# The first unit's first phase in token halves: gate/up of 256 tokens, their down projection with the convolution's tasks, then the other 256

## Chip, cores, metric

The kernel runs on one core of a Trainium2 chip. The metric is device time in microseconds (us); smaller is better. All matrices are bfloat16, sums are float32.

## What is computed

Four layers in a row on x = A_q, of shape (2048 tokens, 576 channels). Layers 1 and 3 are a long convolution with gating, layers 2 and 4 a gated feed-forward network with 4608 hidden channels:

```python
def _A_ref(q, k, v, shift_k, ssm_k, ssm_D):      # q is the layernorm of x
    k_shift = sum over t < 4 of k_pad[:, t:t + S, :] * shift_k[:, 3 - t]
    kv = k_shift * v
    y = causal convolution over the 2048 tokens of kv with ssm_k, per channel (by FFT)
    y = y + kv * ssm_D
    return q * y

def _B_ref(x, w_gate, w_up, w_down):             # x is the layernorm of x
    return (_gelu(x @ w_gate) * (x @ w_up)) @ w_down

x = x + _A_ref(_layernorm(x), A_k, A_v, A_shift_k, A_ssm_k, A_ssm_D)
x = x + _B_ref(_layernorm(x), B_w_gate, B_w_up, B_w_down)
x = x + _A_ref(_layernorm(x), A_k, A_v, A_shift_k, A_ssm_k, A_ssm_D)
x = x + _B_ref(_layernorm(x), B_w_gate, B_w_up, B_w_down)
```

The convolution's result y does not depend on x, so it is computed once, for both convolution layers.

## The kernel before

**Units and phases.** Tokens are taken in four blocks of 512. A unit is one feed-forward layer on one block; there are eight: for each pair of blocks, layer 2 on both and then layer 4 on both. A unit has three phases, each over a third of the hidden channels (12 tiles of 128). A phase is *gate/up* (for each tile, 18 matmuls of 64 rows, gate and up side by side in the array, L1848; half as many columns at a time in the first phase, L1684), the product gelu(gate) * up into the hidden tile `hT` (gelu on ScalarE, L1663 or L1857; the product on VectorE, L1667, L1690 or L1858), and *down* (`down_rows`: for each of four rows of 128 tokens, 24 matmuls of 128 rows and 288 columns, L1723), whose sum is added to `x_c` on VectorE (L1759, L1762, L1754).

**The convolution.** It is done by matrices of 128 x 128 in blocks of 512 tokens: forward transforms on TensorE (in quarters, `quarter`, L284, copied out by ScalarE, L287, and combined by VectorE, L247, L251, L256), products with the filter's transform on VectorE (L361 to L364, L622), and inverse transforms on TensorE (`inverse`, L417, copied to `y` by ScalarE, L423). The opening (`begin`) does the first block; the work of the later blocks is cut into tasks that a planner sets between the feed-forward's instructions. One convolution pair takes a PSUM tile from the pool `cps` (one tile) or, when the planner allows it, from the pool `ps` (three tiles, tag `pr`), which gate/up, down and the transpositions share.

**What sets the order.** The order of every engine's instructions is fixed when the program is built. A planner (`Pace`, `fill`, `run_v`, `run_p`) keeps a modelled time for TensorE, VectorE and ScalarE, with the constants `C_...`, and puts a task in where its inputs should be ready. The constant `H1_AT` is the modelled time from which the transform of the second filter block may begin. Each engine runs its own list in order and waits on semaphores. DMAs are issued from SyncE (weights `wgu` and `wd`, and the transposes of `xn` into `xnT`, L1341) and from GpSimd (the rest).

**The first phase of the first unit** (`wb == 0`). Its input `xnT` comes from transpositions on TensorE (`turn0`, L1483), copied out by ScalarE or VectorE (`copy0`, L1490). Tokens stand in `xnT` in the order `AT0 = (0, 2, 1, 3)`, so that rows 0 and 2, ready first, make the first 256 tokens. `first_half` does gate/up of these for all 12 tiles, in six blocks of two tiles (`half_gu`, 36 matmuls), and sets the transpositions of rows 1 and 3 and the first convolution tasks between the blocks. Then six blocks do the other 256 tokens, with convolution tasks between them, and then `down_rows` does all four rows, with more convolution tasks.

**The second unit's input.** The first inverse transform after the opening (L417, in the first unit's third phase) gives y of the second block. VectorE forms x plus the gated y (L1279, L1286), ScalarE its sum of squares (L1244), GpSimd the root (L1251, L1252), VectorE the norm `xn` (L1316, L1318), and SyncE issues two transposes for each of the four rows into `xnT` (L1341). The second unit's gate/up needs all eight.

**Scratch.** `begin` has its scratch in a pool `s_tmp`, which is closed at its end. The pools of `hT` and of `wd` (down's matrix, a sixth of it in each of three buffers) are opened after it and take its place, so the first three loads of `wd` (L1208) wait for the last readers of that scratch.

Of the kernel before, what the change touches and what calls it, by code (L numbers as in the profile page):

```python
# [15 lines left out]
ACT = mybir.ActivationFunctionType  # L16
# [6 lines left out]
P = 128  # L23
# [8 lines left out]
FG = 4  # L32
NEVER = 1e9

C_GU, C_DN = 1.944, 0.245
C_PR = 1.25
C_BF, C_TB, C_R4 = 0.41, 0.46, 0.77
C_SQ, C_TINY, C_NA, C_NV, C_ROOT, C_NB = 0.85, 0.6, 0.95, 0.74, 1.5, 0.4
# [2 lines left out]
C_TT, C_ST, C_HT, C_H2, C_GELU, C_EVA, C_EVD = 0.76, 0.82, 0.69, 0.7, 0.6, 0.66, 0.76  # L41
LAG = 0.25
AHEAD, CHAINED = 2.0, 2.5
H1_AT = 13.0
LATE = (1, 2)
HOLD, LEAD, HURRY, SPARE = 14.0, 1.8, 2.6, 4.0
LANDED, ENDING, VISIT, EARLY = 9.0, 1.5, 1.6, 1.6
# [40 lines left out]
class Conv:  # L88
# [755 lines left out]
    def begin(self, head, tables):  # L844
# [4 lines left out]
        with ExitStack() as es:  # L849
# [3 lines left out]
            sk9 = tmp.tile([NH, 2, HP * KS], BF16, name="sk9")  # L853
            dv9 = tmp.tile([NH, 2, HP], BF16, name="dv9")
            sk9t = tmp.tile([NH, KS, HP], BF16, name="sk9t")
            hx = tmp.tile([P, RT, D], BF16, name="hx")
            dcol = tmp.tile([P, nd + 1], F32, name="dcol")
            nt = nd - 1
            DW = D - nt * P
            wcol = tmp.tile([P, nt, KS], F32, name="wcol")  # L860
            sx = tmp.tile([P, KS, DW], BF16, name="sx")
            warm = tmp.tile([P, 1], F32, name="warm")
            self.Wx = tmp.tile([P, 2, P], BF16, name="Wx")
            Wn = tmp.tile([P, 2, P], BF16, name="Wn")
            hn = tmp.tile([P, nd + 1, BS], BF16, name="hn")
            hT0 = tmp.tile([P, RT, D], BF16, name="hT0")
            kT = head.scratch([P, nt, RT, P + 2], "kT")
            dg = head.scratch([P, nt, RT, P], "dg")
            kx = tmp.tile([P, RT + KS - 1, DW], BF16, name="kx")
# [9 lines left out]
            nc.vector.memset(kT[:, :, :, 0:2], 0.0)  # L879
            nc.vector.memset(below[:, 0:1], 0.0)  # L880
            nc.vector.tensor_copy(out=below[:, 1:P], in_=self.ident[:, 0:P - 1])
            nc.scalar.activation(out=warm[:], in_=full[:, 0:1], func=ACT.Sqrt)
# [5 lines left out]
            nc.sync.dma_start(out=self.Wx[:], in_=tables[:, 24:26, :])  # L888
# [4 lines left out]
            nc.sync.dma_start(out=self.Td[1].rearrange("(t p) d -> p t d", p=P), in_=hx[:])  # L893
            head.more(2)

            new = lambda: self.psp.tile([P, 2, 512], F32, tag="pr", name="ps")
# [229 lines left out]
            nc.scalar.activation(out=warm[:], in_=head.zero, func=ACT.Gelu_apprx_tanh)  # L1126
            self.keep_y(0, 3, Y[3])
            head.stats(3)
            self.load_v(1, nc.gpsimd)
# [11 lines left out]
def ssm_geglu_kernel(ctx, tc, A_q, A_k, A_v, A_shift_k, A_ssm_k, A_ssm_D, B_x, B_w_gate, B_w_up,  # L1141
# [308 lines left out]
    with tc.manual_schedule():  # L1450
# [136 lines left out]
        def more(k):  # L1587
# [7 lines left out]
        head = SimpleNamespace(  # L1595
            zero=neghalf_t[:], more=more, reserve=reserve0, idle=idle0, stats=stats0, act_stats=act_stats0, half_stats=half_stats0, root_of=root_of0, mean_of=mean_of0, scales=scales0, even_out=even_out0, gate_even=gate_even0, gate=gate0, mean=mean0, sq=sq0, std=std0, norm=norm0, turn=turn0, copy=copy0,
            scratch=lambda shape, name: xtp.tile(shape, BF16, tag="xnT", name=name),
            stay=lambda: xpool.tile([P, RT, 2, D], BF16, tag="x", name="H1"))
        conv.begin(head, tables)

        first_pools = ctx.enter_context(ExitStack())
        hpool = first_pools.enter_context(tc.tile_pool(name="hT", bufs=1))
        dpool = first_pools.enter_context(tc.tile_pool(name="wd", bufs=3))
        for n in range(3):
            load_wd(n)

        def first_half(hT):

            gvars[0][1]["rstd"] = small.tile([P, 1], F32, tag="e_rstd", name="rstd")
            nc.vector.reciprocal(out=gvars[0][1]["rstd"][:], in_=gvars[0][1]["std"])  # L1610
            gate0(1, None, 1)
            mean0(1)
            gate0(3)
            mean0(3)
            for n in range(FP // 2):
                tail = half_gu(hT, n, 0, n < 4)
                t.pe += C_GU
                if n == 3:
                    t.on_dve(C_HT, t.on_act(C_GELU, t.pe + 0.15) + 0.15)
                if n == 0:  # L1620
                    sq0(1)
                    root0(1)
                if n < 4:
                    tail()
                if n == 0:
                    norm0(1)
                if n == 1:
                    sq0(3)
                    conv.put_at(0)
                    root0(3)  # L1630
                elif n in (2, 3, 4):
                    if n == 2:
                        norm0(3)
                        for part, kt in ((1, 0), (0, 1), (1, 1)):
                            conv.apart0(conv.A0, part, kt)
                        conv.together0(conv.A0)
                        conv.put_at(1)
                        load_x(1)
                        t.dve, t.act = t.pe + 3.4, t.pe + 0.6
                    if n < 4:  # L1640
                        conv.run_p()
                    if n > 2:
                        j = 2 * n - 5
                        turn0(j)
                        copy0(j, nc.scalar.copy)
                        t.on_act(1.4, t.pe)
                if n > 3:
                    tail()
                if n == 4:
                    t.dve -= EARLY  # L1650
                if n > 1:
                    fill(t.pe + C_GU + HURRY, False, True)

        two = {}

# [44 lines left out]

        hidden_of = {}

        def down_rows(wb, ph, ui):

            layer, c = units[ui]
            end = ph == NP - 1
            if ui == 0 and end:
                unit0.clear()
            conv.window = t.pe + RT * FP * C_DN - SPARE if wb < WHOLE * NP else -1.0
            hs = hidden_of.pop(ui)  # L1710
            nf = FP * len(hs)
            for j in range(RT):
                acc = psp.tile([P, 2, 512], F32, tag="pr", name="dn")
                last = ui == NU - 1 and end and j == RT - 1
                part = [acc, psp.tile([P, 2, 512], F32, tag="pr", name="dn") if last else acc]
# [75 lines left out]
        for wb, ph, ui, first, final, downs in visits:  # L1791
# [37 lines left out]
            free = deque([0.0] * 3)  # L1829
            if wb == 0:  # L1830
                first_half(hT)
                for n in range(FP // 2):
                    tail = half_gu(hT, n, 1, False)
                    t.pe = max(t.pe, free.popleft()) + C_GU
                    free.append(tail())
                    if n == 0:
                        conv.window = t.pe + 0.6
                    if n % 2:
                        when_due(t.pe, load_wgu, n // 2 + 3)
                    fill(t.pe + lead(FP // 2 - 1 - n), now(), conv.left > 0)  # L1840
            for fi in range(FP if wb else 0):
                n, gi = divmod(wb * FP + fi, FG)
                w = wgu[n]
# [25 lines left out]
                run_made()  # L1869
            if downs is None:  # L1870
                continue
            if pi < WHOLE:
                down_rows(wb, ph, ui)
            else:
                for u in downs:
                    down_rows(wb, ph, u)
# [51 lines left out]
```

## Time and profile before

| | |
|---|---|
| time, median of 3 runs | 906.85 us (906.75 to 907.37) |
| profiled execution | 906.44 us, its span 904.7 us |
| granted TensorE clock | 1.0 |
| TensorE busy | 899.0 us, 99% of the span |
| VectorE busy | 558.3 us, 62% |
| ScalarE busy | 329.5 us, 36% |
| GpSimd busy | 156.8 us, 17% |
| DMA | 132.90 MB, mean 147 GB/s |

The span runs from the first to the last instruction in the profile; 1.74 us of the execution lie around it. In the profile's rows PE is TensorE, PEld its weight loads, DVE VectorE, ACT ScalarE, POOL GpSimd and SP SyncE; L1848 is line 1848 of the kernel. A row of a timeline has the start and the time of a group of equal instructions, then engine, line, operation, output and inputs, shape and count. Starts are counted from the span's start. Instructions of a group can overlap, so a group's time can reach into the next row. In a wait row stand the total, the number of waits and the longest.

### The profile page before, as it was taken

To read this page: it belongs to the slowest core of one execution; us is meant where nothing else is said; L and a number is where in the kernel's file an instruction comes from. 1 tells how busy PE (TensorE), PEld (TensorE's weight loads), DVE (VectorE), ACT (ScalarE), POOL (GpSimd) and SP (SyncE) were. 2 spreads that over 40 slices of the span, in tenths; PEclk is the share of its full clock that TensorE was granted. 3 is DMA by queue.
4 is the path that set the end of the run, shared out by engine and by line. 5 is a ranking of instruction groups with operands and counts; after the bars stand their busy time and mean duration, and the time that the engine had idled before them with its cause. 6 is when DMAs were issued, how large, how long until landed. Compare 5 with 4: busy or idle time off the path is not lost.

```text
span 904.7 us, 19123 instructions
## 1 busy us (share of the span) xinstructions
PE 899.0 (99%) x8133; PEld 525.1 (58%) x8133; DVE 558.3 (62%) x960; ACT 329.5 (36%) x616; POOL 156.8 (17%) x336
## 2 busy tenths in 40 slices
PE   9999999999999999999999999999999999999998
PEld 7875646556466465564654655644444477754466
DVE  8989977678888884887898855443333322023311
ACT  7775455433322264443115133553323323022310
POOL 3323315020223031420104002310000012000000
PEclk9999999999999999999999999999999999999999
DMA  9999987667639219675815501964444431249700
GB/s 274 306 298 315 217 220 145 167 203 157 189 95 260 89 28 180 207 139 138 268 54 136 128 1 40 200 129 106 132 105 132 102 69 28 56 128 225 182 7 20
DMA packets 132075, 132.90 MB, mean 147 GB/s; under 512 B 46139, under 2 KB 123670, under 8 KB 131990
## 3 DMA queue, kind: packets, MB, share of 16 engines
q1 hardware_dynamic: 121728, 94.65, 45.7%
q0 software_dynamic: 10208, 37.02, 12.8%
q8 instruction: 63, 1.03, 0.5%
q14 instruction: 22, 0.18, 0.1%
q10 hardware_dynamic: 54, 0.01, 0.0%
HBM read 108.36 MB, written 12.39 MB: 133 GB/s over the span
## 4 chain that ended last, share of the span: by engine, by line
PE 97%; DVE 2%; issue 0%; ACT 0%; DVEq 0%
PE gu L1848 59%; PE dn L1723 31%; PE gu L1684 3%; PE cps L284 1%; PE ps L417 1%; PE cps L417 1%; PE ps L284 0%; DVE yb L364 0%; DVE prod L361 0%; DVE h L235 0%; DVE prod L363 0%; PE xps L1483 0%; PE cps L903 0%; DVE v L998 0%; DVE wx L961 0%; DVE wx L960 0%
## 5 line engine op out<-in xcount | busy, mean ns | idle before, releaser
L1848 PE MATMUL gu<-xnT,wgu 64*128 64x512 bf16 x4968 | 539.4, 376 | 0.0
L1848 PEld LDWEIGHTS <-wgu 64*128 64x128 bf16 x4968 | 240.2, 94 | 294.3 <-issue 4.3
L1857 ACT ACTIVATE ga<-gu 128x512 f32<-128x512 f32 x258 | 153.9, 597 | 404.1 <-PE gu L1848 395.9
L1858 DVE TENSOR_TENSOR hT<-ga,gu 128x512 bf16<-128x512 f32 x258 | 177.0, 686 | 198.8 <-ACT ga L1857 197.4
L1723 PE MATMUL dn<-wd,hT 128*128 128x288 bf16 x2304 | 290.9, 286 | 0.0
L1723 PEld LDWEIGHTS <-hT 128*128 128x128 bf16 x2304 | 224.1, 98 | 63.0 <-issue 6.4
L1236 POOL TENSOR_SCALAR nm<-s 128x1 f32<-128x1 f32 x56 | 20.3, 362 | 264.7 <-DVE x_c L1754 201.8
L1244 ACT ACTIVATE junk<-x_c,nm 128x576 bf16<-128x576 f32 x48 | 36.9, 770 | 46.0 <-POOL nm L1236 43.9
L1745 DVE TENSOR_TENSOR ob<-x_c,dn 128x576 bf16<-128x576 f32 x15 | 11.3, 754 | 67.6 <-PE dn L1723 67.6
L562 POOL DMA_DIRECT2D hr<-Hd x32 | 17.4, 545 | 117.7 <-DVE prod L363 117.1
L1252 POOL TENSOR_TENSOR rstd<-ve,neghalf_t 128x1 f32<-128x1 f32 x58 | 36.9, 636 | 4.8
L1762 DVE TENSOR_TENSOR x_c<-x_c,dn 128x576 f32<-128x576 f32 x38 | 28.5, 751 | 5.6 <-PE dn L1723 5.2
L1308 ACT ACTIVATE xn<-x_c,nb,rstd 128x576 bf16<-128x576 f32 (+1 forms) x48 | 28.6, 644 | 9.0 <-POOL nb L1256 8.9
L287 ACT COPY eo<-cps 128x576 f32<-128x576 f32 x29 | 18.6, 643 | 27.3 <-PE cps L284 24.1
L1251 POOL TENSOR_SCALAR ve<-ss 128x1 f32<-128x1 f32 x58 | 20.4, 351 | 47.0 <-ACT junk L1244 46.9
L1754 DVE SCALAR_TENSOR_TENSOR x_c<-dn,x_c 128x576 f32<-128x576 f32 x16 | 12.1, 754 | 26.1 <-PE dn L1723 26.1
L1663 ACT ACTIVATE ga<-gu 128x512 bf16<-128x512 f32 x26 | 15.5, 598 | 30.5 <-PE gu L1848 25.9
L1684 PE MATMUL gu<-xnT,wgu 64*128 64x256 bf16 x432 | 24.8, 269 | 0.3 <-ACT xnT L1490 0.3
L432 POOL DMA_DIRECT2D out_dram<-ob x12 | 6.8, 563 | 97.8 <-DVE ob L1745 97.8
L1684 PEld LDWEIGHTS <-wgu 64*128 64x128 bf16 x432 | 21.4, 94 | 3.2 <-issue 1.2
L364 DVE TENSOR_TENSOR prod<-prod 128x576 bf16<-128x576 bf16 x48 | 22.0, 458 | 1.7
L247 DVE SCALAR_TENSOR_TENSOR eo<-eo 128x576 f32<-128x576 f32 x22 | 16.3, 752 | 5.8 <-ACT eo L287 5.8
(182 smaller groups left out, 589.5 us busy)
## 6 DMA issues: line engine op xcount, KB each, us to landing
wgu<-in_B_w_gate_dram SPq DMA_DIRECT2D x45, 576.0 KB, 5.5
wd<-in_B_w_down_dram SPq DMA_DIRECT2D x30, 864.0 KB, 7.9
wgu<-in_B_w_up_dram SPq DMA_DIRECT2D x45, 512.0 KB, 7.3
hr<-Hd POOLq DMA_DIRECT2D x32, 288.0 KB, 4.8
kr<-Kd POOLq DMA_DIRECT2D x24, 288.0 KB, 5.2
Kd<-kc POOLq DMA_DIRECT2D x12, 288.0 KB, 6.5
k<-in_A_k_dram POOLq DMA_DIRECT2D x3, 1008.0 KB, 9.5
wgu<-in_B_w_up_dram SPq DMA_DIRECT2D x45, 64.0 KB, 7.0
```

Source lines behind the costliest of these rows:

```text
L364: nc.vector.tensor_tensor(out=dst, in0=pr[:, 0, :], in1=pr[:, 1, :], op=ALU.subtract if part == 0 else ALU.add)
L1236: nc.gpsimd.tensor_scalar(out=v["nm"][:], in0=v["s"][:], scalar1=-1.0 / D, scalar2=None, op0=ALU.mult)
L1244: nc.scalar.activation(out=junk[:], in_=get_x(), func=ACT.Square, bias=v["nm"][:, 0:1], accum_out=v["ss"][:])
L1251: nc.gpsimd.tensor_scalar(out=ve[:], in0=v["ss"][:], scalar1=1.0 / D, scalar2=EPS, op0=ALU.mult, op1=ALU.add)
L1252: nc.gpsimd.tensor_tensor(out=v["rstd"][:], in0=ve[:], in1=neghalf_t[:, 0:1], op=ALU.pow)
L1308: nc.scalar.activation(out=xn[:, lo:hi], in_=x_c[c][:, j, 0:hi - lo], func=ACT.Identity, scale=v["rstd"][:, 0:1], bias=v["nb"][:, 0:1])
L1684: nc.tensor.matmul(pair[:, s, e * 256:(e + 1) * 256], lhsT=w[r0:r0 + HK, k, gi * P:(gi + 1) * P], rhs=xnT[r0:r0 + HK, blk_of[k], tok], sta ...
L1723: nc.tensor.matmul(part[h][:, h, 0:HW], lhsT=hT[:, f, at * P:(at + 1) * P], rhs=wd[2 * wk + f // WT][:, f % WT, h * HW:(h + 1) * HW], star ...
L1762: nc.vector.tensor_tensor(out=xh, in0=xh, in1=acc[:, :, 0:HW], op=ALU.add)
L1848: nc.tensor.matmul(pair[:, s, :], lhsT=w[r0:r0 + HK, k, gi * P:(gi + 1) * P], rhs=xnT[r0:r0 + HK, b, :], start=(k == 0), stop=(k == NKC - 1))
L1857: nc.scalar.activation(out=ga[:], in_=pair[:, 0, :], func=ACT.Gelu_apprx_tanh)
L1858: nc.vector.tensor_tensor(out=hT[:, fi, :], in0=ga[:], in1=pair[:, 1, :], op=ALU.mult)
```

## The change

Gate/up of the first 256 tokens now runs without other work between its six blocks. After it come the transpositions of rows 1 and 3, then down of rows 0 and 2 with convolution tasks between its matmuls, then gate/up of the other 256 tokens, without convolution tasks on TensorE, and then down of rows 1 and 3 with convolution tasks. `down_rows` gets the rows to do as an argument. The planner counts 0.6 for a row's transposition (`C_TURN`), and `H1_AT` goes from 13 to 11. The hidden tile's pool is opened ahead of `begin`, and the scratch that the opening reads longest (`hx`, `warm`, `Wx`, `Wn`, `hT0`) lies in that tile's place instead of in `s_tmp`.

```diff
-C_GU, C_DN = 1.944, 0.245
+C_GU, C_DN, C_TURN = 1.944, 0.245, 0.6
...
-H1_AT = 13.0
+H1_AT = 11.0
...
-            hx = tmp.tile([P, RT, D], BF16, name="hx")
+            own = head.hidden()[:].rearrange("p f c -> p (f c)")
+            at = [0]
+
+            def lasting(n, m):
+                lo = at[0]
+                at[0] += n * m
+                return own[:, lo:lo + n * m].rearrange("p (n m) -> p n m", n=n)
+            hx = lasting(RT, D)
...
-            warm = tmp.tile([P, 1], F32, name="warm")
-            self.Wx = tmp.tile([P, 2, P], BF16, name="Wx")
-            Wn = tmp.tile([P, 2, P], BF16, name="Wn")
+            warm = lasting(2, 1)[:, 0, :]
+            self.Wx = lasting(2, P)
+            Wn = lasting(2, P)
...
-            hT0 = tmp.tile([P, RT, D], BF16, name="hT0")
+            hT0 = lasting(RT, D)
...
+            hidden=lambda: hpool.tile([P, FP, CH], BF16, tag="hT", name="early"),
...
-        conv.begin(head, tables)
-
         first_pools = ctx.enter_context(ExitStack())
         hpool = first_pools.enter_context(tc.tile_pool(name="hT", bufs=1))
+        conv.begin(head, tables)
...
-                elif n in (2, 3, 4):
-                    if n == 2:
-                        norm0(3)
-                        for part, kt in ((1, 0), (0, 1), (1, 1)):
-                            conv.apart0(conv.A0, part, kt)
-                        conv.together0(conv.A0)
-                        conv.put_at(1)
-                        load_x(1)
-                        t.dve, t.act = t.pe + 3.4, t.pe + 0.6
-                    if n < 4:
-                        conv.run_p()
-                    if n > 2:
-                        j = 2 * n - 5
-                        turn0(j)
-                        copy0(j, nc.scalar.copy)
-                        t.on_act(1.4, t.pe)
+                elif n == 2:
+                    norm0(3)
+                    for part, kt in ((1, 0), (0, 1), (1, 1)):
+                        conv.apart0(conv.A0, part, kt)
+                    conv.together0(conv.A0)
+                    conv.put_at(1)
+                    load_x(1)
+                    t.dve, t.act = t.pe + 3.4, t.pe + 0.6
...
+            for j in (1, 3):
+                turn0(j)
+                t.pe += C_TURN
+                copy0(j, nc.scalar.copy)
+                t.on_act(1.4, t.pe)
+            while made:
+                run_made()
...
-        def down_rows(wb, ph, ui):
+        def down_rows(wb, ph, ui, js=range(RT)):
...
-            for j in range(RT):
+            for j in js:
...
                 first_half(hT)
+                down_rows(wb, ph, ui, (0, 2))
                 for n in range(FP // 2):
                     tail = half_gu(hT, n, 1, False)
                     t.pe = max(t.pe, free.popleft()) + C_GU
                     free.append(tail())
-                    if n == 0:
-                        conv.window = t.pe + 0.6
                     if n % 2:
                         when_due(t.pe, load_wgu, n // 2 + 3)
-                    fill(t.pe + lead(FP // 2 - 1 - n), now(), conv.left > 0)
+                    fill(t.pe + lead(FP // 2 - 1 - n), False, conv.left > 0)
...
-            if pi < WHOLE:
+            if wb == 0:
+                down_rows(wb, ph, ui, (1, 3))
+            elif pi < WHOLE:
                 down_rows(wb, ph, ui)
```

More of the change, by code (lines that the diff above doesn't have):

```diff
@@ L881, in begin @@
             nc.vector.tensor_copy(out=below[:, 1:P], in_=self.ident[:, 0:P - 1])
-            nc.scalar.activation(out=warm[:], in_=full[:, 0:1], func=ACT.Sqrt)
+            nc.scalar.activation(out=warm, in_=full[:, 0:1], func=ACT.Sqrt)
             nc.sync.dma_start(out=hn[:, 0:nd, :], in_=self.hk[0:nd * P, 0:BS].rearrange("(b p) t -> p b t", p=P))
@@ L887, in begin @@
             head.more(0)
-            nc.sync.dma_start(out=self.Wx[:], in_=tables[:, 24:26, :])
+            nc.sync.dma_start(out=self.Wx, in_=tables[:, 24:26, :])
             nc.sync.dma_start(out=self.W[:, 12:24, :], in_=tables[:, 12:24, :])
@@ L892, in begin @@
             head.more(1)
-            nc.sync.dma_start(out=self.Td[1].rearrange("(t p) d -> p t d", p=P), in_=hx[:])
+            nc.sync.dma_start(out=self.Td[1].rearrange("(t p) d -> p t d", p=P), in_=hx)
             head.more(2)
@@ L1125, in begin @@
             head.copy(2, nc.scalar.copy, nc.vector.tensor_copy)
-            nc.scalar.activation(out=warm[:], in_=head.zero, func=ACT.Gelu_apprx_tanh)
+            nc.scalar.activation(out=warm, in_=head.zero, func=ACT.Gelu_apprx_tanh)
             self.keep_y(0, 3, Y[3])
@@ L1709, in down_rows @@
             conv.window = t.pe + RT * FP * C_DN - SPARE if wb < WHOLE * NP else -1.0
-            hs = hidden_of.pop(ui)
+            hs = hidden_of[ui]
+            if js[-1] == RT - 1:
+                hidden_of.pop(ui)
             nf = FP * len(hs)
-            for j in range(RT):
+            for j in js:
                 acc = psp.tile([P, 2, 512], F32, tag="pr", name="dn")
```

## The prediction

> **What bounds the kernel now.** First the page's busy times, then the view of what TensorE (PE) waited for.
>
> ```profile
> PE 899.0 (99%) x8133; PEld 525.1 (58%) x8133; DVE 558.3 (62%) x960; ACT 329.5 (36%) x616; POOL 156.8 (17%) x336
> ```
>
> ```profile
> PE ps L417 <- DVE yb L364: 0.6, 1, 0.6
> PE gu L1684 <- ACT xnT L1490: 0.3, 1, 0.3
> ```
>
> PE is busy for 99% of the span. The waits view has one more row, in the opening; the wait on gate/up (L1684) ends at 33.12 us, and from there PE never waits until the end. So there is no idle time to win. The change can gain only where PE's own work gets shorter, and loses wherever a wait appears. I therefore read PE's timeline around the changed phase (start, busy time, line, count).
>
> ```profile
> 1.25 1.89 PE L903 MATMUL cps<-wx 128*128 128x256 bf16 x8 [1.25 <-DVE below L880]
> ...
> 33.12 8.04 PE L1684 MATMUL gu<-xnT,wgu 64*128 64x256 bf16 x144 [0.31 <-ACT xnT L1490]
> 41.08 0.68 PE L1483 MATMUL xps<-ident,xn 128*128 128x128 bf16 x9
> 41.69 2.14 PE L1684 MATMUL gu<-xnT,wgu 64*128 64x256 bf16 x36
> ...
> 48.44 0.42 PE L284 MATMUL cps<-hT,W 128*128 128x288 bf16 x2
> ...
> 49.03 2.14 PE L1684 MATMUL gu<-xnT,wgu 64*128 64x256 bf16 x36
> 51.11 0.42 PE L284 MATMUL cps<-hT,W 128*128 128x288 bf16 x2
> 51.46 2.14 PE L1684 MATMUL gu<-xnT,wgu 64*128 64x256 bf16 x36
> ...
> 60.84 0.41 PE L284 MATMUL cps<-v,W 128*128 128x288 bf16 x2
> 61.09 2.12 PE L1723 MATMUL dn<-wd,hT 128*128 128x288 bf16 x16
> ...
> 74.90 5.36 PE L1848 MATMUL gu<-xnT,wgu 64*128 64x512 bf16 x48
> ```
>
> Two things are to be seen. Gate/up of two tiles for 256 tokens (36 matmuls) is followed by other work in 2.08 us (49.03 to 51.11), but four such blocks in a row (144) take only 7.96 (33.12 to 41.08). With u for a block and x for leaving the run: u + x = 2.08, 4u + x = 7.96, so u = 1.96 and x = 0.12. And two convolution matmuls between gate/up runs take 0.35 until gate/up goes on (51.11 to 51.46), while between down matmuls they take 0.25 (60.84 to 61.09): entering gate/up costs 0.10. One visit of other work inside gate/up thus costs **0.22 us** beyond its matmuls; inside down it costs nothing.
>
> **The change, part by part.** I take the new order from the built program and the durations from the rows; line numbers are those of the kernel before.
>
> *Visits removed.* Before, the first phase has six such visits (two token-block transpositions, four of the convolution). After, it has one, the first down between the two halves: 5 x 0.22 = 1.1 us. Later the new order has one visit fewer as well (a lone convolution pair in a much later gate/up run): 0.2. Matmul counts are the same. **Gain 1.3 us**; nothing hides it, since PE never waits there.
>
> *Waits added in the first phase.* The transpositions, the first down and the convolution now come right behind the sixth gate/up block, and all want PSUM tiles that ScalarE (ACT) or VectorE (DVE) must empty first.
>
> ```profile
> 44.51 1.18 ACT L1490 COPY xnT<-xps 128x640 bf16<-128x640 bf16 x2 [1.53 <-PE xps L1483]
> ...
> 48.55 0.60 ACT L1663 ACTIVATE ga<-gu 128x512 bf16<-128x512 f32 x1 [0.89 <-PE gu L1684]
> 49.04 0.58 ACT L1664 CAST hT<-gu 128x512 bf16<-128x512 f32 x1
> 49.51 0.66 ACT L287 COPY eo<-cps 128x576 f32<-128x576 f32 x1
> ```
>
> Six blocks end at 33.12 + 6 x 1.96 + 0.12 = 45.00; 18 transpositions (9 took 0.61 less the 0.10) end at 46.02. ACT starts the gelu 0.11 after a block's end (48.44 to 48.55), the copy 0.49 later, which takes 0.58: the tile that the first down needs is free at 46.18. **Wait A: 0.16.** Two down and two convolution matmuls (0.49) bring PE to 46.67. The next convolution matmul takes the tile of the first transposition. ACT is in order: its xnT copies start 0.47 after that last copy began, at 46.07, and take 1.18: 47.25. **Wait B: 0.58.** Behind it on PE stands the rest of the first down; on ACT the convolution's copies queue behind the xnT ones.
>
> ```profile
> 47.63 0.76 DVE L201 TENSOR_TENSOR kvt<-kvt 128x1152 bf16<-128x1152 bf16 x1
> 48.42 0.76 DVE L206 TENSOR_TENSOR v<-kvt,v 128x1152 bf16<-128x1152 bf16 x1
> 49.10 1.42 DVE L196 TENSOR_TENSOR kvt<-k,skc 128x1152 bf16<-128x1152 bf16 x2
> 50.43 0.69 DVE L1667 TENSOR_TENSOR hT<-ga,hT 128x1024 bf16<-128x1024 bf16 x1
> ...
> 64.47 0.82 DVE L1759 SCALAR_TENSOR_TENSOR x_c<-dn,scale_t,x_c 128x576 f32<-128x576 f32 x1 [0.64 <-PE dn L1723]
> 65.21 0.75 DVE L247 SCALAR_TENSOR_TENSOR eo<-eo 128x576 f32<-128x576 f32 x1
> 65.99 1.56 DVE L256 TENSOR_TENSOR kc<-eo 128x288 bf16<-128x288 f32 x4
> ```
>
> Then 46 matmuls of down and convolution at 0.123 (96 in 11.87, a row further down, less the 0.10) end at 52.91, where the next convolution tile waits for DVE's first x_c sum (L1759). DVE's new order from 47.63: L201 until 48.42, L1667 0.69, L206 0.68, two L196 1.33, L201 0.76, L196 0.68 make 52.56, and L1759 0.82 ends at 53.38. **Wait C: 0.47.** Twelve matmuls, the entry to gate/up and one block bring PE to 56.92. One of three PSUM tiles is now held by a convolution pair across the second half, so the second block needs the tile of the second down row. DVE gets to that row after L201 (0.74 + 0.76), two L247 (0.78 each), four L256 (1.56): from 52.56 to 57.18, done at 58.00. **Wait D: 1.08.** Sum 2.3; if the dependent DVE steps run as close as the independent ones (about 0.1 less each) 1.8, if each copy and sum comes 0.2 late 3.0. I take 2.3, since each step has its own row.
>
> The phase then ends at 58.00 + 5 x 1.96 + 0.12 + 66 x 0.123 + 0.10 = 76.14, against 74.90: **+1.2** (-1.1 + 2.3).
>
> *Loads.* The down matrix's loads were held by the scratch in whose place they go; now they follow the previous load.
>
> ```profile
> 34.64 3.55 SPq L1208 DMA_DIRECT2D wd<-in_B_w_down_dram  x3
> ```
>
> ```profile
> DMA to landing us min/median/max: 7.9/12.7/17.5
> ```
>
> The loads' order on SP is unchanged, and on POOL's queue only some 128x1 means change places with transfers. SP's transfers land in the order of issue behind those still under way, so I give the earlier issue nothing; the second third of the matrix is needed at 48.73 (47.25 + 12 x 0.123) and came at about 34.64 + 12.7 = 47.3. The next phase's gate/up weights are issued when the second block frees its buffer, 59.9, and took up to
>
> ```profile
> wgu<-in_B_w_up_dram SPq DMA_DIRECT2D x1, 512.0 KB, 14.3
> ```
>
> so 60.5 + 14.3 = 74.8, under a need at 76.14. The cover is 1.3 us; each us beyond it would be a us of PE.
>
> *The second half has no convolution work on PE.* DVE then only waits for gelu results, its chain ends later, and the new order puts the inverse of the second token block (L417) two gate/up tiles later in the third phase: 10 tiles, then 16 matmuls, one tile, 16 matmuls, one tile, down. Before it was 8, and three tiles behind. What hangs on this is the second unit's input: y, gate, norm (L1316), then DMA transposes into xnT. Chain view, DVE's timeline, SP's queue, the transposes' form:
>
> ```profile
> 125.90 2.07 PE ps L417 x16
> ...
> 132.08 5.93 PE gu L1848 x54
> 138.01 11.87 PE dn L1723 x96
> 149.88 23.42 PE gu L1848 x216
> ```
>
> ```profile
> 135.46 0.81 DVE L1286 SCALAR_TENSOR_TENSOR x_c<-x_c,rstd,x_b 128x576 f32<-128x576 f32 x1
> ...
> 136.20 0.81 DVE L1279 SCALAR_TENSOR_TENSOR x_c<-x_b,nm,y 128x576 f32<-128x576 bf16 x1
> ...
> 141.10 0.76 DVE L1754 SCALAR_TENSOR_TENSOR x_c<-dn,x_c 128x576 f32<-128x576 f32 x1 [1.45 <-PE dn L1723]
> ...
> 141.78 0.57 DVE L1316 TENSOR_SCALAR xn<-x_c,nm,rstd 128x576 bf16<-128x576 f32 x1
> 142.39 0.18 DVE L1318 COPY xn<-xn 128x64 bf16<-128x64 bf16 x1
> ```
>
> ```profile
> 133.19 14.55 SPq L1341 DMA_TRANSPOSE xnT<-xn  x8
> ```
>
> ```profile
> L1341 SPq DMA_TRANSPOSE xnT<-xn x16: 1201/1264/4995, 133.2 to 168.6; - x16
> ```
>
> ```profile
> xnT<-xn SPq DMA_TRANSPOSE x1, 2.5
> ```
>
> Before: the last transpose was issued at 133.19 + 14.55 - 1.26 = 146.48 and landed 2.5 later, 148.98; gate/up of the second unit began at 149.88. The margin was 0.9. After, counted from the inverse's start: PE needs 132.08 - 125.90 = 6.18, one tile 5.93 / 3 = 1.98, down 11.87: it wants xnT at **20.03** (before 23.98). DVE gives the third row's sum (L1286) the same place, 9.56; in the new order L1279 follows at 10.30, L1286 at 11.11, a down sum (L1754) at 11.92, the second row's norm at 12.60, its copy from 13.21 to 13.39. Six transposes of 1.26 follow on SP, the last starts at 19.71 and lands at 22.21. SP reaches the third row at 15.9 and the fourth at 18.4; even with the 6.3 that lay before between a sum (135.46) and a norm (141.78), they are ready at 15.9 and 17.4, so SP sets the pace. **Wait E: 2.2 us.** At 1.20 a transpose 1.8; if one takes the 4.995 of the same row, 5.9. I take 2.2: most are near the median. What stands behind it: the weight load and the third unit's transposes on SP, which have a whole phase to spare.
>
> **Sum.** -1.3 + 2.3 + 2.2 = +3.2 us. The profiled execution took 906.44 us with a span of 904.7; +3.2 gives 909.6. The median shown, 906.85, is 0.41 above it: **910.0 us**.
>
> **Rivals.** A measurement of this kernel can tell about 0.2% (1.8 us) from no change.
>
> *No wait E.* If the norm of the second row comes 2.2 earlier against PE, the second unit starts as before: -1.3 + 2.3 = +1.0, 907.9. For it: before there was a margin. Against: SP's six transposes alone take 7.6 of the 20.03.
>
> *The other side: only the visits count.* Place: PE's changes between 64-row gate/up and 128-row work. Price -1.3, 905.5. It decides if ACT's four xnT copies are out by 46.67, DVE's second sum by 56.92 and E is gone. Against: ACT and DVE take their work in order, and the sum of rows is 0.6 and 1.1 late.
>
> *PE slows after a long wait.* At the opening eight matmuls of 256 columns took 1.89, 1.08 columns per ns, against 288 in 0.123, 2.3: half rate after idleness. If wait E did this again for such a stretch, half of 1.89 is lost, at least 0.9: 910.9. Against: after the 0.3 wait before 33.12 the blocks run at full rate. The Trainium skill, "TensorE: Matmul & The Clock Gate", section "HAM oscillation — how this bites in real kernels", says that idle gaps beyond about 3.4 us put the array back to half clock; by that rule a 2.2 us wait does not, and an estimate from its window, if E grew past it, would be 1.7 us more. No run so far shows it.
>
> *The down matrix comes late.* If its second part lands like the last (17.5), at 52.1 instead of 48.73, PE waits 3.4, part of C and D goes: about 912.5.
>
> **How the numbers follow.** Forecast 0.55 (its own range 909.1 to 912.2); no E 0.15; visits only 0.10; slow restart 0.08; late matrix 0.05; a gain that I don't see 0.05, a loss 0.02. Range 905.5 to 912.2: it reaches the no-change cases below; left out are the unseen ones, the late matrix and E's far end, together under 0.2. Slower: 0.55 + 0.08 + 0.05 + 0.02 = 0.70; same 0.15 + 0.10 = 0.25; faster 0.05.
>
> **What would show it.** In the changed profile PE's waits should list ACT xnT (0.6) and DVE x_c (0.5 and 1.1) between 46 and 58 us, and a DMA xnT wait of about 2 at the second unit's start near 153; gate/up runs of 216 without visits. The forecast is wrong if the second unit starts before 151 us, if the first phase ends before 75.5, or if new waits stand after 160.

## The result, and the profile after

| | before | changed |
|---|---|---|
| median | 906.76 us (906.43 to 907.37, 6 runs) | 910.66 us (909.35 to 913.53, 6 runs) |
| profiled execution | 906.44, span 904.7 | 910.34, span 908.6 |

The ratio is 1.0047, 95% interval 1.0036 to 1.0059: slower, as forecast (910.0, range 905.5 to 912.2). A second, later set of runs gave 910.29 (5 runs) against 906.93 (15 runs), ratio 1.0043 (1.0030 to 1.0056).

First the page's busy times and what TensorE waited for, in the changed kernel. Line numbers are those of that kernel, 6 to 8 higher than before.

```profile
PE 899.4 (99%) x8133; PEld 527.5 (58%) x8133; DVE 558.2 (61%) x959; ACT 331.7 (37%) x618; POOL 161.2 (18%) x336
```

```profile
PE gu L1855 <- DMA xnT<-xn: 1.9, 2, 1.2
PE cps L910 <- DVE below L887: 1.2, 1, 1.2
PE gu L1690 <- DVE x_c L1767: 0.6, 1, 0.6
PE ps L417 <- DVE yb L364: 0.6, 1, 0.6
PE ps L284 <- ACT xnT L1497: 0.4, 1, 0.4
PE gu L1690 <- ACT xnT L1497: 0.3, 1, 0.3
PE ps L937 <- DMA k<-in_A_k_dram: 0.3, 1, 0.3
PE ps L284 <- DVE x_c L1767: 0.2, 1, 0.2
```

The matmuls take what they took (899.4 against 899.0 busy). New are the waits for the transposed input (term E), for `x_c` (D and C), for the xnT copies (B), and one for `k` in the opening that the prediction did not have. TensorE's timeline shows where each stands.

```profile
34.16 11.97 PE L1690 MATMUL gu<-xnT,wgu 64*128 64x256 bf16 x216 [0.31 <-ACT xnT L1497]
46.06 1.18 PE L1490 MATMUL xps<-ident,xn 128*128 128x128 bf16 x18
47.29 0.41 PE L1731 MATMUL dn<-wd,hT 128*128 128x288 bf16 x2
47.53 0.41 PE L284 MATMUL cps<-hT,W 128*128 128x288 bf16 x2
48.38 0.41 PE L284 MATMUL ps<-hT,W 128*128 128x288 bf16 x2 [0.44 <-ACT xnT L1497]
...
53.52 0.65 PE L1731 MATMUL dn<-wd,hT 128*128 128x288 bf16 x4
54.35 0.40 PE L284 MATMUL ps<-v,W 128*128 128x288 bf16 x2 [0.18 <-DVE x_c L1767]
...
55.92 2.14 PE L1690 MATMUL gu<-xnT,wgu 64*128 64x256 bf16 x36
58.69 10.00 PE L1690 MATMUL gu<-xnT,wgu 64*128 64x256 bf16 x180 [0.63 <-DVE x_c L1767]
...
76.81 3.41 PE L1855 MATMUL gu<-xnT,wgu 64*128 64x512 bf16 x30
...
131.62 2.13 PE L417 MATMUL ps<-yb,W 128*128 128x288 bf16 x16
...
139.85 11.93 PE L1731 MATMUL dn<-wd,hT 128*128 128x288 bf16 x96
152.98 0.39 PE L1855 MATMUL gu<-xnT,wgu 64*128 64x512 bf16 x2 [1.19 <-DMA xnT<-xn]
154.13 23.27 PE L1855 MATMUL gu<-xnT,wgu 64*128 64x512 bf16 x214 [0.76 <-DMA xnT<-xn]
177.33 0.42 PE L1731 MATMUL dn<-wd,hT 128*128 128x288 bf16 x2
```

Read it against the same rows of before, stage by stage:

- *Opening.* The first gate/up begins at 34.16, before at 33.12: **+1.04**, not predicted. It differs from one execution to the next (below) and is no part of the change.
- *First phase.* 34.16 to 76.81 is 42.65; before 33.12 to 74.90 is 41.78: **+0.87** (predicted 1.2).
- *Wait E.* From the start of down (139.85) to the start of the next unit's down (177.33) are 37.48; before 35.29 (the same rows, 11.87 of down and 23.42 of gate/up): **+2.19** (predicted 2.2). The two wait rows list only 1.19 + 0.76 of it.
- *Later.* The lone convolution pair that before stands in a gate/up run at 408.40 is not there: **-0.2**. No new wait stands behind 160 us.

The sum, 1.04 + 0.87 + 2.19 - 0.2 = 3.90, is the difference of the spans (908.6 - 904.7).

### The profile page after: what moved, and what is told of

Its sections match the earlier page's. It is cut to its first block, busy times and chain, and to the rows that moved or that the text cites. A ratio compares the mean times of both kernels' runs of the same rounds, so it can differ in the third digit from the quotient of the medians.

```text
span 908.6 us, 19127 instructions
## 1 busy us (share of the span) xinstructions
PE 899.4 (99%) x8133; PEld 527.5 (58%) x8133; DVE 558.2 (61%) x959; ACT 331.7 (37%) x618; POOL 161.2 (18%) x336
## 3 DMA queue, kind: packets, MB, share of 16 engines
q0 software_dynamic: 10208, 37.02, 12.6%
## 4 chain that ended last, share of the span: by engine, by line
PE 92%; DVE 2%; SPq 2%; DMA 2%; issue 1%; POOL 0%; ACT 0%; ACTq 0%; DVEq 0%
PE gu L1855 59%; PE dn L1731 29%; DMA hT<-Td 1%; PE gu L1690 1%; SPq L1209 1%; PE cps L284 1%; SPq L898 1%; DVE kvt L196 1%; DMA dv<-in_A_ssm_D_dram 0%; PE ps L417 0%; PE cps L417 0%; PE ps L284 0%; SPq L1207 0%; DVE kvt L201 0%; SPq L1208 0%
## 5 line engine op out<-in xcount | busy, mean ns | idle before, releaser
L1259 POOL TENSOR_TENSOR rstd<-ve,neghalf_t 128x1 f32<-128x1 f32 x58 | 39.9, 689 | 4.8
L1770 DVE TENSOR_TENSOR x_c<-x_c,dn 128x576 f32<-128x576 f32 x38 | 28.5, 751 | 10.1 <-PE dn L1731 10.0
L1293 DVE SCALAR_TENSOR_TENSOR x_c<-g_t,rstd,x_c 128x576 f32<-128x576 f32 x16 | 13.1, 816 | 8.9 <-POOL rstd L1259 8.7
```

The source lines that it names most:

```text
L1259: nc.gpsimd.tensor_tensor(out=v["rstd"][:], in0=ve[:], in1=neghalf_t[:, 0:1], op=ALU.pow)
L1770: nc.vector.tensor_tensor(out=xh, in0=xh, in1=acc[:, :, 0:HW], op=ALU.add)
```

## Experiments

**The two parts apart.** First the scratch's new place in the kernel before, the split left out:

```diff
-            hx = tmp.tile([P, RT, D], BF16, name="hx")
+            hx = lasting(RT, D)
... (Wx, Wn, warm, hT0 and the hidden tile's pool likewise)
```

> The kernel before with one part of the change: the opening's lasting scratch in the hidden tile's place. The order of TensorE's matmuls is that of before. In the changed kernel's profile gate/up begins 1.04 us later than before (34.16 against 33.12); nothing in the prediction said so. If the place of the scratch does this, this kernel takes about 907.8 us and gate/up begins near 34.2. If the opening varies from one execution to the next, it takes 906.8 (plus or minus 0.3) and gate/up begins wherever that execution's transfers let it. An earlier load of the down matrix is worth nothing by both.

Measured: 906.67 (11 runs) against 906.61 (23 runs), ratio 1.0001 (0.9992 to 1.0009); gate/up began at 33.24. The scratch's place costs nothing and brings nothing that these runs can tell.

Then the split without the scratch's move (the reverse of that diff, in the changed kernel):

> The changed kernel with the scratch back in its old pool: the other part alone, with TensorE's order of the change. If the place of the scratch costs nothing, the time is that of the change, 910.7; if it costs the 1.04 us of the opening, 909.6. The down matrix is then loaded as late as before; its second third came at about 47.3 to 48.5 us and is needed at 48.7, so that up to 1 us more wait at the first down (L1725 or near it) is possible, which the scratch's move would then have been there to avoid: 911.7.

Measured: 910.0 (5 runs), ratio 1.0033 (1.0021 to 1.0045), with waits B to E of the changed kernel. All of the loss is the split's. The down matrix, loaded as late as before, was in time: no row for `wd` among the waits. And although the scratch lay in its old place, gate/up began at 34.15, so that the opening's 1.04 is not the scratch's either.

**The opening.** Two things differ there between profiles. One is a load: in the first profile of the changed kernel `k` came late, and the matmuls that follow stand 0.4 us later than before.

```profile
4.82 0.64 PE L937 MATMUL ps<-k,below 128*128 128x384 bf16 x2 [0.27 <-DMA k<-in_A_k_dram]
...
8.00 1.69 PE L831 MATMUL cps<-dg,kT 128*128 128x512 bf16 x7
```

The other is the rate at which the same matmuls ran. For six of the profiles, the start of the first matmuls on `k` (L930 or L937), the time of the first seven matmuls of L831 (512 columns each), and the start of gate/up, in us:

| profile | on `k` | L831 x7 | gate/up begins |
|---|---|---|---|
| before | 4.35 | 1.07 | 33.12 |
| changed | 4.82 | 1.69 | 34.16 |
| changed, second profile (below) | 4.40 | 1.89 | 34.18 |
| changed, third profile (below) | 4.45 | 1.05 | 33.13 |
| scratch alone | 4.39 | 1.12 | 33.24 |
| split alone | 4.44 | 1.89 | 34.15 |

The same kernel shows 33.13, 34.16 and 34.18. In the second profile the first seven take 1.68 until the next row starts, a later seven of the same line 0.88: the opening's matmuls run at half rate at first and change to the full rate at a moment that differs between executions. That alone made the second profile 1.05 later than the third; in the first, 0.43 of the 1.04 is the late load (L831 starts at 8.00 instead of 7.57). None of it hangs on the change. It is not all that varies: one execution of the scratch alone took 909.09, 2.4 over its median, and what it lost is not known.

The Trainium skill, "TensorE: Matmul & The Clock Gate", section "Part 1: The HAM clock gate (the "warmup" mystery)", says that the window over which activity is counted runs freely, so that the moment of the change varies by half a us to either side; the spread of 0.84 us in one row of matmuls fits that.

**Wait E by itself.** The kernel before, with the inverse of the second token block held back by two gate/up tiles, and nothing else touched (a later convolution pair moves along, as in the changed kernel):

```diff
+LATER = 93.0
...
-            self.Pq.extend((zs, 2 * cost, inv_two(mts), m) for mts in ((0, 1), (2, 3)))
+            self.Pq.extend((lambda: max(zs(), LATER), 2 * cost, inv_two(mts), m) for mts in ((0, 1), (2, 3)))
```

> The kernel before with one condition more: the inverse of the second token block may not begin before a modelled time, which puts it behind 10 gate/up tiles of the third phase, as in the changed kernel, and leaves the first phase alone. By the prediction's term E the second unit's gate/up waits for the transposes of xnT by about 2.0 to 2.2 us, and the time is 908.8 to 909.0 (one later convolution pair moves too, 0.2). If the wait would be hidden, or was a matter of the first phase's lateness, 906.8. If a wait of this kind can also slow TensorE for a stretch, single executions lie 1.8 to 3.5 us above the others, with a granted clock under 1.0.

Measured: 909.69 (6 runs, 908.82 to 911.25), ratio 1.0033 (1.0021 to 1.0045); the profiled execution 909.0. Its timeline on TensorE (gate/up began at 33.38):

```profile
138.21 11.93 PE L1724 MATMUL dn<-wd,hT 128*128 128x288 bf16 x96
151.60 0.39 PE L1849 MATMUL gu<-xnT,wgu 64*128 64x512 bf16 x2 [1.46 <-DMA xnT<-xn]
152.77 23.27 PE L1849 MATMUL gu<-xnT,wgu 64*128 64x512 bf16 x214 [0.77 <-DMA xnT<-xn]
175.97 0.42 PE L1724 MATMUL dn<-wd,hT 128*128 128x288 bf16 x2
```

138.21 to 175.97 is 37.76, 2.47 over before. Holding the inverse back two tiles makes the whole wait, without any change to the first phase: E is shown to be that.

**What makes the inverse late.** The changed kernel with the convolution's tasks let into the second half's gate/up again:

```diff
+                    if n == 0:
+                        conv.window = t.pe + 0.6
...
-                    fill(t.pe + lead(FP // 2 - 1 - n), False, conv.left > 0)
+                    fill(t.pe + lead(FP // 2 - 1 - n), now(), conv.left > 0)
```

> The changed kernel with the convolution's tasks again let into the second half's gate/up (three visits), which brings the inverse of the second block from behind tile 10 to behind tile 7 of the third phase. By the prediction's terms: wait E (2.0) gone, three visits of 0.22 back (0.7), wait D (0.6) gone or moved: 908.8 to 909.4 with the opening as in the changed kernel, 907.8 to 908.4 with the opening as before. If the second half without tasks is not what makes the inverse late, or the time was lost elsewhere, 910.7 or more.

Measured: 907.75 (11 runs), ratio 1.0012 (1.0003 to 1.0020). The waits that are left beside those of before, and the rows at the second unit:

```profile
PE ps L284 <- ACT xnT L1497: 0.4, 1, 0.4
...
PE ps L284 <- DVE x_c L1767: 0.2, 1, 0.2
```

```profile
124.82 2.13 PE L417 MATMUL ps<-yb,W 128*128 128x288 bf16 x16
...
150.74 23.48 PE L1857 MATMUL gu<-xnT,wgu 64*128 64x512 bf16 x216
```

The inverse now comes before 125 us, the 216 matmuls run without a wait, and D is gone too: the convolution pair that held a PSUM tile across the second half there now does its second quarter at 57.08, behind the first block (in the changed kernel at 68.88). Its first phase, 33.25 to 75.83, is 42.58, as long as the changed kernel's: three visits took the place of D. So keeping the tasks out of the second half makes E, which is most of the loss.

**Longer waits.** The kernel before again, with the inverse three tiles late, and inside down (`LATER = 95.0` and `98.0`):

> The kernel before with the inverse of the second token block three gate/up tiles late (behind tile 11) instead of two. The two-tile version took 909.7, its wait E 2.2 in the profiled run. By the prediction's chain (SyncE's six transposes of 1.26 us behind the second row's norm set the pace) TensorE needs the input 1.98 sooner after the inverse begins, so the wait is 4.2 us if VectorE is no earlier, 2.8 if it gains the 1.6 us for which it waited for a gelu result there: 909.4 to 910.8 at full clock. If a TensorE that waits longer comes back at half rate for a stretch of 3 to 4 us (each us of it costs half a us), 911 to 912.8 and a granted clock of 0.998, in more executions than with two tiles.

> The kernel before with the inverse of the second block only inside the third phase's down. TensorE then has 16 + 16 inverse matmuls and 90 down matmuls (122 x 0.123 = 15.0 us) between the inverse's start and the second unit's gate/up; by the chain of norms and transposes the input comes 20.8 to 22.2 after the inverse's start, so the wait is 5.8 to 7.2 us: 912.4 to 913.8 at full clock. A wait of this length should show by itself whether TensorE comes back slow: the 216 gate/up matmuls behind it take 23.4 us from start to end at full rate; at half rate for 3.4 us they take 25.1. If the transposes, not VectorE, hold it, eight transposes stand without gaps on SyncE's queue.

Measured: three tiles late 909.8 (5 runs, 909.28 to 912.56), ratio 1.0037 (1.0023 to 1.0050); inside down 916.28 (one run). Stretches of two us on TensorE in the profile of the first (span of the stretch, busy time, granted clock, DMA share, GB/s):

```profile
150.00:152.00 2.00, 0.24 (x2) 1.00 0.55 118
152.00:154.00 2.00, 0.93 (x4) 0.56 0.51 86
154.00:156.00 2.00, 2.00 (x12) 0.50 0.94 283
156.00:158.00 2.00, 2.00 (x13) 0.50 1.09 388
158.00:160.00 2.00, 2.00 (x16) 0.73 1.06 412
160.00:162.00 2.00, 2.00 (x22) 1.00 1.20 150
```

and the rows behind the wait in the second:

```profile
157.55 25.77 PE L1849 MATMUL gu<-xnT,wgu 64*128 64x512 bf16 x216 [7.58 <-DMA xnT<-xn]
183.25 0.42 PE L1724 MATMUL dn<-wd,hT 128*128 128x288 bf16 x2
```

Three tiles late, the wait rows sum to 2.8 us, the lower end of what was expected, and TensorE ran at half clock for 6.8 us. It began in the first gap: in stretches of half a us the clock is 1.00 until 152.0, 0.76 in the next and 0.50 from 152.5, and the two matmuls behind the gap of 2.20 start at 152.45. From down to down are 179.53 - 138.32 = 41.21, 5.92 over before: 3.27 until the 214 matmuls start, and 2.65 because they take 25.85 instead of 23.20. Three of the five executions lay at 909.3 to 909.8 with a clock of 1.0, so that it does not come each time. Behind the wait of 7.58 us the 216 matmuls took 25.70 instead of 23.42: 2.3 us lost. The wait itself was a little longer than the 7.2 expected; together with the half clock and an opening 0.5 late (33.65) that covers the 2.5 by which the time exceeds the 913.8 expected at full clock. The eight transposes did not stand without gaps: they took 12.36 us instead of 8 x 1.26 = 10.1, the last row's norm (150.86) waited 2.23 for its root, and so the chain of that row, and not SyncE's queue, held the last two.

**The changed kernel again,** unaltered, in two further profiles:

> The changed kernel itself once more, beside the one above and the kernel before. Its opening should begin gate/up somewhere between 33.1 and 34.2 us, as that execution's warm-up lets it (1.04 us of the first profile's 3.9 are then no part of the change), its first phase should take 42.65 and wait E about 2.1. Median 910.0 to 910.7 if the change costs what the parts cost (first phase 0.9, wait E 2.1, late visit -0.2, and in some executions a half clock behind wait E); if an execution with a granted clock below 1.0 is the one profiled, the stretch behind wait E shows 0.50 for some us.

> The changed kernel, one more profiled execution: does half clock stand behind wait E here? With it the span is 2 to 3.5 us over one without it (907.6), without it gate/up's 214 matmuls take 23.2 us from start to start of the next row.

Measured: 910.29 (5 runs, 910.23 to 911.93) and 911.02 (one run). The profile of the five (910.33) has the late opening (34.18) and the full clock behind E, like the first. The last is the other way round:

```profile
150.00:152.00 2.00, 0.82 (x9) 1.00 0.45 99
152.00:154.00 2.00, 1.24 (x12) 1.00 0.47 82
154.00:156.00 2.00, 2.00 (x14) 0.55 1.02 253
156.00:158.00 2.00, 2.00 (x14) 0.59 1.13 231
158.00:160.00 2.00, 2.00 (x22) 1.00 1.07 225
```

Here gate/up began at 33.13, E's wait rows are the same to 0.01, and behind them the 214 matmuls took 153.09 to 177.98, 24.89 instead of 23.20: **1.69 us** lost, with the clock at half for 3.4 us, from about 154.2 on (a mean of 0.55 over two us is 1.8 us at 0.50, one of 0.59 is 1.6). With first phase 0.87, E 2.19 and -0.2 that makes 4.55, its span 909.2 - 904.7 = 4.5. So the change itself costs 2.9 us in each of the three profiles (0.87 + 2.19 - 0.2; its fastest run, 909.35, is 2.92 over the fastest of before). On top, two of the profiles pay about 1.0 in the opening and one 1.7 behind E. The other executions were not profiled: the two slowest, 913.3 and 913.5, are 4 us over the fastest, with a mean granted clock of 0.998, and how their 4 us divide stays open.

The Trainium skill, "TensorE: Matmul & The Clock Gate", section "HAM oscillation — how this bites in real kernels", puts the fall to half clock at idle gaps beyond about 3.4 us. The profile above disagrees: half clock followed gaps of 1.18 and 0.76 us, with two matmuls between them, in this execution, and not in the two others; in no other stretch of this profile (of 20 us each) was the granted clock below 1.0. Three tiles late it fell inside a gap of 2.20. The loss of 1.69 us agrees with half of that page's window.

**Shortening E.** The changed kernel, its matmul order untouched; ScalarE squares the second row earlier, and VectorE takes its norm ahead of the fourth row's gate:

```diff
-            tasks += [norm_v(i) for i in {1: (0,), 3: (1, 2, 3)}.get(j, ())]
+            tasks += [norm_v(i) for i in {1: (0,), 2: (1,), 3: (2, 3)}.get(j, ())]
... (and run_aq may look 1 us further ahead in the third phase)
```

> The changed kernel, TensorE's order untouched; in the third phase ScalarE takes the square sum of the second row ahead of the second pair's y copies (not behind the last gelu), and VectorE its norm ahead of the fourth row's gate. If wait E is set by SyncE's six transposes behind the second row's norm (145.1 us in the changed kernel's profile), that norm now comes at about 142.9, the last row's at 148.5, the last transpose is issued at 149.8 and lands at 152.3 against a need at 151.8: the wait shrinks from 2.0 to 0.5 and the time from 910.7 to 909.1 or less. If the wait hangs on something else (the landing of a transpose, the last row's norm), it stays near 2 and the time at 910.7.

Measured: 909.21 (6 runs), ratio 1.0028 (1.0017 to 1.0040). From down to down 176.61 - 139.78 = 36.83: E is 1.54, not 0.5. VectorE's norms of the second and of the last row:

```profile
141.92 0.58 DVE L1323 TENSOR_SCALAR xn<-x_c,nm,rstd 128x576 bf16<-128x576 f32 x1
...
148.80 0.58 DVE L1323 TENSOR_SCALAR xn<-x_c,nm,rstd 128x576 bf16<-128x576 f32 x1 [2.16 <-POOL rstd L1259]
```

The second row's norm was as early as planned (144.26 in the changed kernel), but the last row's came 1.2 later than its 147.63 there: ScalarE and GpSimd had first squared and rooted a row of the first unit, whose sum VectorE now took earlier. By this reading the pace went over from SyncE's transposes to the last row's root. To try it, the last row's gate was put ahead of that sum:

```diff
-                        fill(t.pe + (HURRY if hurry() else 1.5), True, conv.left > 0)
+                        fill(t.pe + (HURRY if hurry() else 2.6 if ui == 0 and end and j == 0 else 1.5), True, conv.left > 0)
```

> The version with the early second norm, and besides VectorE takes the last row's gate (L1293) ahead of down's first sum (L1762), so that ScalarE and GpSimd square and root the last row ahead of a row of the first unit. In the early-norm version the last row's norm stood at 148.80, waiting 2.16 us for its root, and wait E had shrunk only from 2.2 to 1.5. If the last row's root was what held it, its norm now comes at about 146.8, the last transpose is issued near 149.0 and lands near 151.5, ahead of the need at 151.7: wait E is 0 to 0.3, the time 907.6 to 908.5 (before + first phase 0.9 - late visit 0.2, and up to 1.0 in the opening), and no half clock behind it. If the transposes themselves set a floor (eight of 1.26 with the landing), E stays above 1 and the time at 909.2.

Measured: 912.02 (12 runs, 907.50 to 916.96), ratio 1.0055 (1.0036 to 1.0075). Waits of the profiled execution (914.05), and VectorE's row behind the longest:

```profile
PE ps L284 <- DVE hT L1867: 3.6, 1, 3.6
...
PE gu L1857 <- DMA xnT<-xn: 0.2, 1, 0.2
```

```profile
176.67 1.43 DVE L196 TENSOR_TENSOR kvt<-k,skc 128x1152 bf16<-128x1152 bf16 x2 [4.64 <-DMA k<-in_A_k_dram]
```

E is down to 0.2 in the list, 0.39 by starts of rows (174.49 - 138.81 - 35.29). Its chain is the one described, with the last row's norm at 146.57, and there is no half clock behind it. But only the fastest of the 12 executions, 907.50, came as low as expected; the profiled one lost more elsewhere. The load of `k` for the third block was issued at 159.57 and landed 17.1 us later; in the changed kernel it was issued at 160.63 and took 7.7. VectorE stood 4.64 us in front of it, with a gate/up product behind it in its queue, and TensorE 3.60 for that product's PSUM tile; then half clock again (0.91 over 164 to 200 us).

Why this load was slow is open. Counted from the start of gate/up in the opening (33.13 here, 34.16 in the changed kernel) it was issued at the same place (126.44 and 126.47), while the third unit's transposes, which run beside it, began 0.96 sooner (121.17 instead of 122.13). But in the early-norm version it follows the first of these by the same 5.27 us (155.85, 161.12; here 154.30, 159.57), and it landed after 9.4 there.

**The first phase.** To the version with tasks in the second half, first some room for the xnT copies, then an earlier sum:

```diff
+            conv.spare_free = max(conv.spare_free, t.pe + 1.0)
... (second step, besides)
-                        fill(t.pe + (HURRY if hurry() else 1.5), True, conv.left > 0)
+                        fill(t.pe + (1.2 if js[-1] == 2 else HURRY if hurry() else 1.5), True, conv.left > 0)
```

> The version with tasks in the second half (907.75 with the inverse behind tile 7), and besides the convolution's second pair is held back about 1 us in the first down, so that it does not ask for a PSUM tile that ScalarE's xnT copies still hold. Wait B (0.43) should go from TensorE's waits; if nothing behind it takes its place the time is 907.3, and what is left against before is wait C (0.2) and the entries into gate/up. If VectorE's first x_c sum sets that stretch anyway, wait C grows by as much, and the time stays 907.7.

> The version with tasks in the second half and room for the xnT copies (908.1 median, 907.4 in its profiled run, first phase 42.5 us), and besides VectorE looks less far ahead in the first down, so that its sum of the first down row comes two convolution steps (L201, L196: 1.46 us) sooner; the other engines' orders are untouched. If waits B and C, one behind the other, are what the first phase loses, no wait for x_c is left (the sum is done near 51.9, the tile is wanted at 53.0) and the first phase takes 41.6 to 41.8 us, no longer than before: 906.5 in the profiled run, within 0.1% of the kernel before. If VectorE's chain holds TensorE at its next dependence (the convolution's sums now 0.8 later), a new wait stands at L284 or in the second half, and the time stays near 907.4.

Measured: 908.11 (11 runs), ratio 1.0011 (1.0002 to 1.0020), and 906.99 (11 runs) against 906.93 (15 runs), ratio 1.0002 (0.9993 to 1.0011). The waits of TensorE in the first:

```profile
PE ps L284 <- DVE x_c L1768: 0.5, 1, 0.5
```

and all of them in the second, with its first phase:

```profile
PE cps L910 <- DVE below L887: 1.2, 1, 1.2
PE ps L417 <- DVE yb L364: 0.6, 1, 0.6
PE gu L1691 <- ACT xnT L1497: 0.3, 1, 0.3
```

```profile
33.26 11.97 PE L1691 MATMUL gu<-xnT,wgu 64*128 64x256 bf16 x216 [0.31 <-ACT xnT L1497]
...
75.10 5.14 PE L1858 MATMUL gu<-xnT,wgu 64*128 64x512 bf16 x46
```

With B gone the phase stayed at 42.57. C grew from 0.2 to 0.5, and 0.3 went to a wait that TensorE's list does not show, because it is its weight loads (PEld) that wait, for the product of the sixth block, which VectorE takes behind a convolution step. It is there in the second version as well:

```profile
49.12 1.34 PEld L1732 LDWEIGHTS <-hT 128*128 128x128 bf16 x12 [0.43 <-DVE hT L1674]
```

The 20 down matmuls around it take 2.75 us (47.85 to 50.60) instead of 20 x 0.123 = 2.46. In the changed kernel B covers it: 26 down matmuls take 3.19 there, at 0.123 each. So B, C and this wait stood one behind the other, and only when VectorE takes its sum two steps sooner does the phase shrink, to 41.84. That is before's length (41.78), although four visits instead of six should make it shorter: the 0.29 above and wait A (0.2) take up what the two visits save. This version ties with the kernel before; none beats it. An earlier product of the sixth block, which would take away the 0.29, was not tried.

## Why the prediction was right

- *Visits, -1.1 here.* The six blocks in a row took 34.16 to 46.06, 11.90, against 6 x 1.96 + 0.12 = 11.88: right.
- *Wait A, 0.16.* No wait row names it, but the 18 transpositions and the start of down took 1.23 instead of 1.02, and down began 0.05 behind the end of the copy of which the step spoke (46.66 + 0.58): 0.2.
- *Wait B, 0.58.* 47.53 and two matmuls (0.24) to 48.38: 0.61, the row lists 0.44.
- *Wait C, 0.47.* 53.52 and four matmuls (0.49) to 54.35: 0.34. *Wait D, 1.08.* 55.92 and a block (1.96) to 58.69: 0.81. VectorE's steps ran closer than their rows one by one (from the first sum to the second 57.82 - 53.49 = 4.33, worked out as 4.62), which was the lower bound's reason (1.8). A to D sum to 1.96, less 1.1 is the measured 0.86.
- *Wait E, 2.2.* Inverse two tiles later, the second row's norm 12.6 behind it (144.26 - 131.62), six transposes, the input 22.2 behind it by the forecast: gate/up went on at 154.13, 22.5 behind. Measured 2.19. Shown by the late inverse alone (2.47) and by the runs that took its parts away.
- *Loads and the down matrix at no cost:* right, also with the matrix loaded late. *No E, visits only, late matrix:* did not happen.
- *The sum* was +3.2, and the part of the change that each profiled execution pays is 2.9: C and D were 0.1 and 0.3 too large. The medians (910.66, 910.29) still lie above the forecast, and the profiles show two things outside the sum that do this. The opening's rate was taken as fixed. And the rival "PE slows after a long wait", given 0.08 and a price of 0.9 as an alternative to the sum, comes on top of it in a part of the executions, with 1.69, behind waits of the very size that the forecast had itself. Its argument against was the wait of 0.3 us before gate/up, which is too short to tell. How much each weighs in the median is not shown, so that a median within 0.7 us of the forecast is in part luck: the sum was a little too large, and what it left out made up for that.
- *The range.* The upper end of the forecast's own range, 912.2, is not worked out from its terms: a sum of waits of 3.0 instead of 2.3 gives 910.7, and the slowest transpose (E at 5.9) 913.7. Two of the first six executions, 913.3 and 913.5, lie above it.

## What to carry to other kernels

Taking work out of one engine's stream moves the work that fed another: here 0.22 us per visit were saved, but the visits had fed VectorE's chain, which without them came two gate/up tiles late at a deadline some 80 us on. Follow the chain from a moved task to its next deadline, and read waits from starts of rows rather than from the wait list, which showed 1.95 of 2.19 us and nothing of a wait that stood at the weight loads. A wait that is cured hands the pace to the next one, sometimes to a worse one: measure each step.

## What the hardware showed that was not expected

- Half clock behind short waits: 3.4 us of it, beginning about 1 us after gaps of 1.18 and 0.76 us, in one of three profiles of the same kernel; 6.8 us of it, beginning inside a gap of 2.20.
- In the opening the clock column says 1.00 throughout, while seven matmuls took 1.05 in one execution and 1.89 in another; there only the durations tell the rate.
- A load of `k` that took 7.7 us in one order took 17.1 in another, issued at the same distance from the opening's end; the cause is open.
